# First q and k loads of a fused attention and FFN kernel: from cast loads on GpSimd to f32 loads on SyncE and ScalarE

## The chip, the cores and the metric

The kernel runs on one core of a Trainium2 chip. Its time is in microseconds (us) of the device. The times given are the median of several executions; the profile is of one further execution, whose own time stands beside its span.

## The reference

Windowed attention over 8 batches of 8 heads with 576 tokens of 64 elements, and a feed-forward network (FFN) with a squared ReLU on its output. Heads 0 to 3 look back over 32 tokens, heads 4 to 7 over every fourth token of the last 128.

```python
def _attn_ref(q, k, v):                    # q, k, v: (8, 8, 576, 64) float32
    scores = scale * np.matmul(q, k.transpose(0, 1, 3, 2))
    rel = pos[:, None] - pos[None, :]
    mask_plain = (rel >= 0) & (rel < 32)
    mask_dil = (rel >= 0) & (rel < 128) & (rel % 4 == 0)
    scores = np.where(masks[None], scores, -1000000000.0)   # plain: heads 0-3, dilated: 4-7
    attn = np.exp(scores - np.max(scores, axis=-1, keepdims=True))
    attn = attn / (np.sum(attn, axis=-1, keepdims=True) + 1e-09)
    return np.matmul(attn, v)

x = attn_out.transpose(0, 2, 1, 3).reshape(4608, 512)
h = np.maximum(x @ w_in, 0.0)              # w_in: (512, 2048)
out = h * h @ w_out                        # w_out: (2048, 512)
```

## The kernel before, in words

All matmuls are in bf16. The FFN works through 4608 tokens in eleven chunks, four of 256 tokens and then seven of 512. A chunk has "groups": `g1` multiplies x by pieces of w_in (line 673), takes the ReLU on ScalarE (L684) and the square on VectorE (L685); `g2` multiplies by w_out (L708), copies the sum out of PSUM (L714) and stores it (L647, SyncE). The attention of a batch is cut into small steps, by pair of heads `e` (0 to 3: two heads each, pairs 0 and 1 plain, 2 and 3 dilated), which stand between the FFN groups of the batch before.

The order of the work is written out by hand. The string `PROGRAM` (L21) holds codes, cut by `|`: the codes of the first stretch run before the first FFN group, those of stretch g + 1 after group g. Nothing else reorders instructions: each engine executes its own in the order in which they are issued here.

The codes that matter:

- `L0:q001` is `load_qk` of batch 0, part 0 (tokens 0 to 255), pairs 0 and 1: one load of q and one of k (L161). `L0:q023` is pairs 2 and 3, `q1..` part 1 (tokens 256 to 575), `L0:v..` are loads of v (L178 to L197), `i0` to `i3` the four pieces of w_in (L770), `o0` to `o3` of w_out (L775). All of these are on GpSimd's queue, which casts f32 to bf16 on the way.
- `T10` transposes q and k of pair 1, part 0, on TensorE into PSUM (L505); `T20q`, `T20k` one of them; `C10a` copies the result to SBUF, q's half on ScalarE (`a`) or VectorE (`v`) at L519 and k's on VectorE (L520), or both at once (L512).
- `B` puts the mask as a bias into PSUM (L535), `S` adds the scores (L554), `E` takes the exponential (L562, for part 1 with a mask on VectorE, L565), `P` multiplies by v (L592), `D` sums the rows (L608), `L` and `X` give the reciprocal on ScalarE (L615, L618), `M` writes the quotient to `xT`, the FFN's input (L625).
- `w9` and `W6` are idle matmuls (L475): so many products of a zeroed tile `idle` with itself into a spare PSUM tile, `w` with 512 columns, `W` with 256. `W5+11` puts them into the PSUM tile of S11 instead, ahead of the exponential that reads it.
- `h` casts v of the plain heads (part 0) from f32 into `vbd[0]` (L797). Those rows come by four plain f32 loads, two on SyncE and two on ScalarE (L739), into a tile that VectorE first writes one column of (L736), after the masks `mk` have landed (L723, ScalarE's first load).
- `u`, `m` build masks on ScalarE, `n` and `z` zero halves of `kbd` and `vbd`.
- Later codes such as `3o1` or `4k0` are steps of a batch: batch 3, the part-0 product with v (`o`) of pair 1; batch 4, k's copies (`k`) of pair 0, with `l` and `h` for one half each and `a` for ScalarE.

Four copies on ScalarE (L734) zero the unused halves of `vbd[0]`: two of 64x1152 and two of 64x128. `xx[0]` and `xx[1]` hold transposed q and k by batch; `xx[1]` is first written for batch 3. PSUM has four buffers of the pool `ps_f` ("pf"), two of `ps_a` ("pa"), one each of "po" and "pd". The FFN's first accumulators are taken from "pf" after S21, S31, S01 and S11.

The first FFN groups run in the order 0, 1 (w_in's first piece), 2, 3 (second piece), 16 (first piece, the second chunk), 4, 5 (third piece), 17 to 21, 6, 7 (fourth piece), and so on.

Of the kernel before, what the change touches and what calls it, by code (L numbers as in the profile page):

```python
# [12 lines left out]
RES = 4  # L13
# [5 lines left out]


PROGRAM = (  # L21
    "L0:q001 L0:q023 L0:q101 L0:q123 L0:v0d L0:i0 L0:v1dr L0:i1 L0:v1p L0:i2 L0:i3 L0:o0 L0:o1 L0:o2 L0:o3 "
    "L1:q00123 z y L1:v0dp L1:q10123 L1:v1dpr w9 T00 C00a T10 C10a B00 B10 W2 S00 E00 B20 W1 S10 E10 u B30 W3 "
    "T20q W6 T20k C20v T30 C30v h W3 S20 E20 W2 S30 E30 T01 C01v T11 C11a W4 P00 P10 D00 D10 L00 T21 C21v T31 "
    "C31v W6 X00 M00 P20 P30 D20 D30 L20 X20 M20 S21 S31 E21 E31 S01 S11 W5+11 E01 E11 | | P21 P31 D21 D31 L21 "
    "X21 M21 L31 X31 M31 | | P01 P11 D01 D11 L01 X01 M01 L11 X11 M11 | | | | | | | | | | | | | m n | | | | | "
    "L2:q00123 L2:q10123 | 1q1 1q3 | 1q2f 1k2f | 1k1a 1v3 | 1a2 | 1v2 1k0a 1q0v | 1o2 | 1a0 1a1 | 1k3 1o0 1o1f "
    "| 1a3 1Q0 | 1K0 1o3 | 1Q1 1K1 | 1Q2 | 1b0 | | 1Q3 1K2 L2:vwpdr L3:q00123 L3:q10123 | L2:x | | 2q0 | | 2k0 "
    "1V2 | 1b2 1p0 | 1b1 1V3 1K3 | | 1p2 1p1f | 2a0 1b3 | 2k1l 2o0 1p3f 2b0 2k1h | 2q1 2k2 L3:x | | 2q2 2p0 "
    "L3:vwpdr 2a1 | | | 2b1 | 2o1 2a2 2v2 2q3 | | 2p1f | 2k3 | 2b2 2o2 | 2v3 | 2a3 2p2f L4:q10123 | 2b3 2o3 | "  # L30
    "3k1 | 2p3 | 3q1v L4:q00123 | 3k0l | 3a1 | 3k0h | | 3o1 3k2l | 3q0 | 3k2h 3v2 | | | 3a0 | 3b1 3k3 | | | "
    "3p1 L4:x 3q2 L4:vwpdr | | 3b0 | 3a2 3q3 3o0 4k0 | | | 3o2 3b2 | | 3p0 3v3 | 4q1 3a3 | 3p2 4q2 4q0 | "
    "L5:q10123 3b3 | 3o3 | 4k1 | | L5:q00123 3p3 4k2 4k3 4a0 L5:vwpdr | | | 4b0 | | 4q3 | | 4o0 | | | 4a2 4v2 "
    "| 4b2 | 4a3 L5:x 4a1 | 4o2 | | | 4p2 L6:q00123 4v3 | | 4b1 | | 4p0 | | 4p1 | 5q0 5k0 | 4b3 | | | | 4o1 | "
    "| 5k2 L6:q10123 4o3 | 5q2 5k1 | | 4p3 | 5q1 |"
)


# [25 lines left out]
def kernel(  # L64
# [85 lines left out]
    def staged(b: int, nm: str):  # L150


        t = rb[STAGE[b]][nm]
        return t[:, :].rearrange("p (a h x) -> p a h x", h=H, a=2)
# [324 lines left out]
    def first_step(code: str):  # L479
# [54 lines left out]
            for x, (to, rhs) in enumerate(adds):  # L534
                nc.tensor.matmul(to, ident, rhs, start=(x == 0), stop=False, skip_group_check=True)  # L535
        elif what == "S":
            ps = ps_f.tile([P, 512], f32, name="pf") if part else first["S", e, part]
            if part == 0:
                pts[e] = p_pool.tile([P, NB * 96], bf16, name="pt")
            bl = blocks(0, e, part)  # L540
# [109 lines left out]
    def ffn_groups(tk0: int, nt: int):  # L650

        early = NT <= tk0 <= 2 * NT
        h2 = h2_pool.tile([P, NF, NT], bf16, name="h2T")
        per = NT // nt
        kts = (0, 2, 1, 3) if tk0 >= NT else (0, 1, 2, 3) if tk0 == 0 else (2, 3, 0, 1)
        cut = 3 if tk0 >= NT else 2
        cur, acc = {}, {}

        cuts = [(0, nt)] if tk0 // RING == (tk0 + nt - 1) // RING else [(0, -tk0 % RING), (-tk0 % RING, nt)]

        def mm1(u, ks):
            if u not in acc:
                acc[u] = ps_f.tile([P, NT], f32, name="pf")
            for x in range(per):
                f = per * u + x
                piece = max(y for y in range(len(w_in_sb)) if w_cuts[y] <= P * f)
                c0 = 512 * (f // 4) + f % 4 - w_cuts[piece]
                for kt in ks:  # L670
                    for y0, y1 in cuts:
                        t0 = (tk0 + y0) % RING
                        nc.tensor.matmul(  # L673
                            acc[u][:, nt * x + y0 : nt * x + y1],
                            w_in_sb[piece][:, kt, c0 : c0 + 509 : 4],
                            xT[:, kt, t0 : t0 + y1 - y0],
                            start=(kt == kts[0] and x == 0 and y0 == 0),
                            stop=(kt == kts[-1] and x == per - 1 and y1 == nt),
                            skip_group_check=True,
                        )  # L680
            if ks[-1] != kts[-1]:
                return
            hv = h2[:, per * u : per * u + per, 0:nt]
            nc.scalar.activation(hv, acc[u][:, :].rearrange("p (x n) -> p x n", x=per), ACT.Relu)  # L684
            nc.vector.tensor_tensor(out=hv, in0=hv, in1=hv, op=ALU.mult)  # L685

        def g1(i):
            if i < 2 and tk0 < NT:
                for u in range(2):
                    mm1(u, kts[2 * i : 2 * i + 2])  # L690
            elif i < 2 and early:
                for u in (2 * i, 2 * i + 1):
                    mm1(u, kts[:cut])
            elif i < 4 and early:
                for u in (2 * i - 4, 2 * i - 3):
                    mm1(u, kts[cut:])
            else:
                mm1(i, kts)

        def g2(m, part):  # L700
            last = tk0 + P * (m + 1) == NTOK
            if part == 0 or last and part == 2:
                cur[m] = ps_f.tile([P, DM], f32, name="pf")

            c0, c1 = (DM // 2 * (part // 2), DM // 2 * (part // 2 + 1)) if last else (0, DM)
            f0, f1 = (NF // 2 * (part % 2), NF // 2 * (part % 2 + 1)) if last else (4 * part, 4 * part + 4)
            for f in range(f0, f1):
                nc.tensor.matmul(  # L708
                    cur[m][:, c0:c1], h2[:, f, P * m : P * m + P], w_out_sb[:, f, c0:c1],
                    start=(f == 0), stop=(f == NF - 1),  # L710
                )
            if f1 == NF:
                osb = osb_pool.tile([P, DM], f32, name="osb")
                nc.scalar.copy(osb[:, c0:c1], cur[m][:, c0:c1])  # L714
                for x in (c0, DM // 2) if c1 - c0 == DM and tk0 == NTOK - NT else (c0,):
                    store(osb, tk0 + P * m, x, DM // 2 if x < min(c1, DM // 2) and tk0 == NTOK - NT else c1)

        return [lambda i=i: g1(i) for i in range(NF // per)] + [
            lambda m=m, part=part: g2(m, part) for m in range(nt // P) for part in range(4)
        ]  # L720

# [5 lines left out]
        nc.vector.memset(t[64:128, :, :, 0:64], 0.0)  # L727

    nc.vector.memset(idle[:, :], 0.0)
    for es, bs in ((slice(0, NE // 2), slice(0, NB)), (slice(NE // 2, NE), slice(8, NB))):  # L730
        for hl in range(2):
            to = vbd[0][64 * hl : 64 * hl + 64, es, bs, 64 - 64 * hl : 128 - 64 * hl]
            none = idle[64 * hl : 64 * hl + 64, 0:64].unsqueeze(1).unsqueeze(1).broadcast_to(list(to.shape))
            nc.scalar.copy(to, none)  # L734
    plain = osb_pool.tile([P, DM], f32, name="osb")[:, :].rearrange("p (e i d) -> p e i d", e=2, d=D)
    nc.vector.tensor_copy(plain[:, :, 0, 0:1], mk[:, 0:2].unsqueeze(2))  # L736
    for e, engine in enumerate((nc.sync, nc.scalar)):
# [47 lines left out]
    def run(code):  # L785
        if code == "y":
            for nm in "qk":
                nc.gpsimd.memset(staged(1, nm)[64:80, 0, :, :], 0.0)
                nc.gpsimd.memset(staged(2, nm)[64:80, 0, 0 : H // 2, :], 0.0)
        elif code == "z":  # L790
            nc.gpsimd.memset(vbd[1][0:64, :, :, 64:128], 0.0)
            nc.gpsimd.memset(vbd[1][64:128, :, :, 0:64], 0.0)
        elif code in "mu":
            masks(int(code == "u"))
        elif code == "h":
            for rows in sides:
                nc.vector.tensor_copy(vbd[0][rows, 0:2, 0:4, rows], plain[rows, :, :, :])  # L797
        elif code == "n":
            zero_halves(kbd)
            zero_halves(vbd[0][:, NE // 2 :, 0:8, :])  # L800
        elif code[0] in "wW":
            n, _, at = code[1:].partition("+")
            turn(int(n), 512 if code[0] == "w" else 256, [int(x) for x in at])
        elif code[0] in "TCBSEPDXM" or code[0] == "L" and code[2:3] != ":":
            first_step(code)
        elif code[0] != "L":
            step(int(code[0]), code[1:])
        else:
            b, what, part, which = int(code[1]), code[3], code[4:5], code[5:]
            if what == "q":  # L810
                load_qk(b, None if part == "w" else int(part), [int(e) for e in which])
            elif what == "x":
                cross_all(b)
            elif what == "v":
                load_v(b, [0, 1] if part == "w" else [int(part)], which)
            else:
                (load_w_in if what == "i" else load_w_out)(int(part))
# [67 lines left out]
```

## Time and profile before

| | |
|---|---|
| median of 7 runs | 310.26 us (309.8 to 312.5) |
| the profiled execution's own time | 311.11 us |
| its span | 309.3 us |
| TensorE matmuls busy | 300.5 us (97%), 2545 |
| TensorE weight loads busy | 188.0 us (61%) |
| VectorE busy | 195.4 us (63%) |
| ScalarE busy | 196.6 us (64%) |
| GpSimd busy | 94.0 us (30%) |
| DMA | 35.05 MB moved, mean 113 GB/s |
| chain that ended last | PE 85%, DMA 5%, GpSimd 2%, VectorE 2%, ScalarE 2% |

The busy times are unions over the span; engines work side by side, so they don't add up to it. PE is TensorE, PEld its weight loads, DVE VectorE, ACT ScalarE, POOL GpSimd, SP SyncE; a `q` behind an engine (ACTq, SPq) marks its queue issuing a load. A line of the timeline has the start and the length in us, engine, source line, operation and tiles, and in brackets how long the engine had stood idle before and what ended that. A line of the windows has the stretch, its length, the busy time of each engine with its instructions, the granted clock of TensorE, the mean share of the 16 DMA engines in use and the GB/s that they wrote. Loads with a cast write half of the bytes that they read.

### The profile page before, as it was taken

What the parts mean: (1) busy time and instruction counts of PE and PEld (TensorE: products, weight loads), DVE (VectorE), ACT (ScalarE), POOL (GpSimd) and SP (SyncE); (2) the same over time, 40 slices, a digit from 0 to 9 for tenths busy, and PEclk for the clock granted to TensorE, in tenths of its full rate; (3) what the DMA queues carried; (4) which work ended last, traced back from release to release, by engine and by line L of the source; (5) the groups of instructions that cost most, each with busy time, mean ns of one, the idle gap of its engine ahead of it and who ended that gap; (6) DMA issues with size and microseconds to landing.
All of it is one profiled execution on the core that took longest, in us unless ns stands there. A gap on an engine that the chain in (4) does not pass through costs nothing.

```text
span 309.3 us, 6792 instructions
## 1 busy us (share of the span) xinstructions
PE 300.5 (97%) x2545; PEld 188.0 (61%) x2577; DVE 195.4 (63%) x637; ACT 196.6 (64%) x421; POOL 94.0 (30%) x138
## 2 busy tenths in 40 slices
PE   7998999999999999999999999999999999999995
PEld 3788756868755555555599555555555555445544
DVE  1555566998988979975798469946995334104400
ACT  7587658859869765795388547854686456216611
POOL 8679785564236254601551051000000000000000
PEclk9999999999999999999999999999999999999999
DMA  7999999999999989999799985601200210121012
GB/s 108 197 169 212 204 134 183 175 128 224 154 110 202 159 130 187 152 137 173 104 127 135 154 125 87 107 11 59 68 3 0 70 69 0 32 72 34 2 53 83
DMA packets 80288, 35.05 MB, mean 113 GB/s; under 512 B 49920, under 2 KB 75648, under 8 KB 80256
## 3 DMA queue, kind: packets, MB, share of 16 engines
q0 software_dynamic: 46592, 18.23, 52.2%
q1 hardware_dynamic: 32976, 16.06, 28.4%
q8 instruction: 20, 0.33, 0.5%
q10 hardware_dynamic: 688, 0.33, 0.5%
q14 instruction: 12, 0.10, 0.1%
HBM read 36.90 MB, written 9.44 MB: 150 GB/s over the span
## 4 chain that ended last, share of the span: by engine, by line
PE 85%; DMA 5%; POOL 2%; DVE 2%; ACT 2%; issue 2%; ACTq 0%; POOLq 0%
PE pf L708 38%; PE pf L673 38%; DMA w_in<-in_moe_w_in_dram 5%; PE po L421 3%; PE pd L423 2%; PE pa L312 2%; PE pa L318 1%; PE pa L236 1%; POOL qb L161 1%; POOL kb L161 1%; DVE qT L256 1%; ACT rec L425 1%; ACT rec L426 1%; DVE kbd L260 1%; DVE xT L436 0%
## 5 line engine op out<-in xcount | busy, mean ns | idle before, releaser
L673 PE MATMUL pf<-xT,w_in 128*128 128x256 bf16 (+1 forms) x758 | 132.0, 325 | 1.4 <-DMA w_in<-in_moe_w_in_dram 0.9
L708 PE MATMUL pf<-w_out_sb,h2T 128*128 128x512 bf16 (+1 forms) x570 | 130.7, 373 | 1.2
L673 PEld LDWEIGHTS <-w_in 128*128 128x128 bf16 x768 | 82.3, 114 | 36.0 <-DMA w_in<-in_moe_w_in_dram 1.2
L684 ACT ACTIVATE h2T<-pf 128x512 bf16<-128x512 f32 x144 | 83.7, 597 | 25.3 <-PE pf L673 24.6
L708 PEld LDWEIGHTS <-h2T 128*128 128x128 bf16 x592 | 54.3, 98 | 53.5
L685 DVE TENSOR_TENSOR h2T<-h2T 128x512 bf16<-128x512 bf16 x144 | 58.0, 422 | 39.9 <-ACT h2T L684 38.7
L714 ACT COPY osb<-pf 128x512 f32<-128x512 f32 (+1 forms) x37 | 21.2, 572 | 43.7 <-PE pf L708 37.8
L436 DVE TENSOR_TENSOR xT<-po,rec 128x288 bf16<-128x288 f32 (+2 forms) x51 | 23.1, 454 | 32.0 <-ACT rec L426 31.5
L178 POOL DMA_DIRECT2D vbd<-in_v_dram x36 | 25.7, 733 | 41.3 <-PE pd L423 37.7
L425 ACT ACTIVATE rec<-pd 128x288 f32<-128x288 f32 (+2 forms) x51 | 21.0, 411 | 23.0 <-PE pd L423 23.0
L322 ACT ACTIVATE pt<-pa 128x352 bf16<-128x352 f32 (+6 forms) x56 | 27.6, 499 | 6.6 <-PE pa L312 3.7
L426 ACT ACTIVATE rec<-rec 128x288 f32<-128x288 f32 (+2 forms) x56 | 24.8, 444 | 1.8
L421 PEld LDWEIGHTS <-vbd 128*128 128x128 bf16 x286 | 17.1, 97 | 9.8 <-issue 0.7
L256 DVE COPY qT<-xx 64x288 bf16<-64x288 bf16 x84 | 21.0, 250 | 1.1
L191 POOL DMA_DIRECT2D vd<-in_v_dram x24 | 14.5, 617 | 16.9 <-DMA kb<-in_k_dram 9.6
L260 DVE COPY kbd<-xx 64x288 bf16<-64x288 bf16 x40 | 18.8, 471 | 0.6
L161 POOL DMA_DIRECT2D qb<-in_q_dram x18 | 12.9, 717 | 18.9 <-DMA xx<-qb 17.2
L421 PE MATMUL po<-pt,vbd 128*128 128x32 bf16 (+3 forms) x256 | 17.5, 198 | 0.4 <-DVE xT L436 0.4
L423 PE MATMUL pd<-pt,mk 128*128 128x32 bf16 (+6 forms) x150 | 15.9, 204 | 0.0
L197 POOL DMA_DIRECT2D vbd<-in_v_dram x16 | 9.7, 609 | 12.6 <-PE pd L423 5.1
L161 POOL DMA_DIRECT2D kb<-in_k_dram x18 | 12.7, 707 | 1.1 <-DMA kb<-in_k_dram 0.6
L312 PE MATMUL pa<-qT,kbd 128*128 128x96 bf16 (+2 forms) x146 | 12.2, 201 | 0.1
(95 smaller groups left out, 235.4 us busy)
## 6 DMA issues: line engine op xcount, KB each, us to landing
out_dram<-osb SPq DMA_DIRECT2D x18, 128.0 KB, 2.7
qb<-in_q_dram POOLq DMA_DIRECT2D x7, 320.0 KB, 7.2
kb<-in_k_dram POOLq DMA_DIRECT2D x7, 320.0 KB, 9.3
vd<-in_v_dram POOLq DMA_DIRECT2D x32, 64.0 KB, 7.1
w_in<-in_moe_w_in_dram POOLq DMA_DIRECT2D x4, 512.0 KB, 8.2
w_out_sb<-in_moe_w_out_dram POOLq DMA_DIRECT2D x4, 512.0 KB, 12.8
qb<-in_q_dram POOLq DMA_DIRECT2D x7, 256.0 KB, 7.4
kb<-in_k_dram POOLq DMA_DIRECT2D x7, 256.0 KB, 9.1
```

Of the source, the lines that this page charges most:

```text
L161: nc.gpsimd.dma_start(t[0:n, part, hs, :], src[b, hs, t0 : t0 + RES * n, :].rearrange("h (p r) d -> p h (r d)", r=RES))
L178: nc.gpsimd.dma_start(dst[rows, e, i0:i1, rows], v[b, 2 * e + hl, 64 * i0 : 64 * i1, :].rearrange("(i p) d -> p i d", p=64),)
L256: copy(qT[rows, e, :, m0 : m0 + n].rearrange("p (c j) m -> p j c m", j=2)[:, jj, :, :], src)
L322: nc.scalar.activation(pt[:, off : off + n], ps[:, 0:n], ACT.Exp, scale=SCALE)
L421: nc.tensor.matmul(oo, vb[:, e, i, :], rh, start=(x == 0), stop=(x == len(mms) - 1), skip_group_check=True)
L425: nc.scalar.activation(rec[:, 0:n], d[:, 0:n], ACT.Ln)
L426: nc.scalar.activation(rec[:, 0:n], rec[:, 0:n], ACT.Exp, scale=-1.0)
L436: nc.vector.tensor_tensor(out=tok, in0=o if o is o3 else o[:, 0:n], in1=rec if o is o3 else rec[:, 0:n], op=ALU.mult)
L673: nc.tensor.matmul(acc[u][:, nt * x + y0 : nt * x + y1], w_in_sb[piece][:, kt, c0 : c0 + 509 : 4], xT[:, kt, t0 : t0 + y1 - y0], start=(kt ...
L684: nc.scalar.activation(hv, acc[u][:, :].rearrange("p (x n) -> p x n", x=per), ACT.Relu)
L685: nc.vector.tensor_tensor(out=hv, in0=hv, in1=hv, op=ALU.mult)
L708: nc.tensor.matmul(cur[m][:, c0:c1], h2[:, f, P * m : P * m + P], w_out_sb[:, f, c0:c1], start=(f == 0), stop=(f == NF - 1),)
```

## The change

- The first loads of batch 0, `L0:q001` (q and k, pairs 0 and 1, part 0), are taken out of GpSimd's queue. In their place four plain f32 loads, of two heads each, go to the still unused `xx[1]`: q's two on SyncE, k's two on ScalarE. Casts (`c00`, `c10` on VectorE for q, `c01`, `c11` on ScalarE for k) bring them to where the cast loads wrote.
- One of four zero copies stays on ScalarE; three become memsets on VectorE (`g`, after `C10a`).
- Idle matmuls: `w9` becomes `w7`; `W4` and the second `W6` go; `W5+11` becomes `W2+31`.
- S01 and S11 run before X00 and take their PSUM from "pa"; E01 and E11 come before P20.
- In the middle, `3a1`, `3o1`, `3q2`, `3k3` and `4q1` stand up to nine groups elsewhere (stretches 67 to 91); `4k0` is cut in two halves, both on ScalarE, and stands later.
- The copy of the last row block out of PSUM is shared by ScalarE and VectorE; the stores of two more row blocks are cut in two halves of columns.

```diff
-    "L0:q001 L0:q023 L0:q101 L0:q123 L0:v0d L0:i0 L0:v1dr L0:i1 L0:v1p L0:i2 L0:i3 L0:o0 L0:o1 L0:o2 L0:o3 "
-    "L1:q00123 z y L1:v0dp L1:q10123 L1:v1dpr w9 T00 C00a T10 C10a B00 B10 W2 S00 E00 B20 W1 S10 E10 u B30 W3 "
-    "T20q W6 T20k C20v T30 C30v h W3 S20 E20 W2 S30 E30 T01 C01v T11 C11a W4 P00 P10 D00 D10 L00 T21 C21v T31 "
-    "C31v W6 X00 M00 P20 P30 D20 D30 L20 X20 M20 S21 S31 E21 E31 S01 S11 W5+11 E01 E11 | | P21 P31 D21 D31 L21 "
...
+    "L0:q023 L0:q101 L0:q123 L0:v0d L0:i0 L0:v1dr L0:i1 L0:v1p L0:i2 L0:i3 L0:o0 L0:o1 L0:o2 L0:o3 L1:q00123 z "
+    "y L1:v0dp L1:q10123 L1:v1dpr w7 c00 c01 T00 C00a c10 c11 T10 C10a g B00 B10 W2 S00 E00 B20 W1 S10 E10 u "
+    "B30 W3 T20q W6 T20k C20v T30 C30v h W3 S20 E20 W2 S30 E30 T01 C01v T11 C11a P00 P10 D00 D10 L00 T21 C21v "
+    "T31 C31v S01 S11 X00 M00 E01 E11 P20 P30 D20 D30 L20 X20 M20 S21 S31 W2+31 E21 E31 | | P21 P31 D21 D31 "
...
-            ps = ps_f.tile([P, 512], f32, name="pf") if part else first["S", e, part]
+            if part:
+                pool, nm = (ps_f, "pf") if dil else (ps_a, "pa")
+                first["S", e, part] = pool.tile([P, 512], f32, name=nm)
+            ps = first["S", e, part]
...
-                nc.scalar.copy(osb[:, c0:c1], cur[m][:, c0:c1])
-                for x in (c0, DM // 2) if c1 - c0 == DM and tk0 == NTOK - NT else (c0,):
-                    store(osb, tk0 + P * m, x, DM // 2 if x < min(c1, DM // 2) and tk0 == NTOK - NT else c1)
+                mid = (c0 + c1) // 2 if last else c1
+                nc.scalar.copy(osb[:, c0:mid], cur[m][:, c0:mid])
+                if last:
+                    nc.vector.tensor_copy(osb[:, mid:c1], cur[m][:, mid:c1])
+                for x in (c0, DM // 2) if c1 - c0 == DM and tk0 + P * m >= NTOK - NT - 256 else (c0,):
+                    store(osb, tk0 + P * m, x, DM // 2 if x < min(c1, DM // 2) and tk0 + P * m >= NTOK - NT - 256 else c1)
...
     nc.vector.memset(idle[:, :], 0.0)
-    for es, bs in ((slice(0, NE // 2), slice(0, NB)), (slice(NE // 2, NE), slice(8, NB))):
-        for hl in range(2):
-            to = vbd[0][64 * hl : 64 * hl + 64, es, bs, 64 - 64 * hl : 128 - 64 * hl]
+    raw = [
+        xx[1][0:64, x, 0 : 4 * RES * D * 2].bitcast(f32).rearrange("p (h d) -> p h d", h=4) for x in range(2)
+    ]
+    for e in range(2):
+        for x, (src, engine) in enumerate(((q, nc.sync), (k, nc.scalar))):
+            engine.dma_start(
+                raw[x][:, 2 * e : 2 * e + 2, :],
+                src[0, 2 * e : 2 * e + 2, 0:256, :].rearrange("h (p r) d -> p h (r d)", r=RES),
+            )
+
+    def zeros(hl, es, bs, act):
+        to = vbd[0][64 * hl : 64 * hl + 64, es, bs, 64 - 64 * hl : 128 - 64 * hl]
+        if act:
             none = idle[64 * hl : 64 * hl + 64, 0:64].unsqueeze(1).unsqueeze(1).broadcast_to(list(to.shape))
             nc.scalar.copy(to, none)
+        else:
+            nc.vector.memset(to, 0.0)
+
+    zeros(0, slice(0, NE // 2), slice(0, NB), True)
...
+        elif code == "g":
+            zeros(1, slice(0, NE // 2), slice(0, NB), False)
+            for hl in range(2):
+                zeros(hl, slice(NE // 2, NE), slice(8, NB), False)
+        elif code[0] == "c":
+            e, x = int(code[1]), int(code[2])
+            hs = slice(2 * e, 2 * e + 2)
+            (nc.scalar.copy if x else nc.vector.tensor_copy)(staged(0, "qk"[x])[0:64, 0, hs, :], raw[x][:, hs, :])
```

The new loads and the one zero copy stand ahead of the v loads of L739 on SyncE and ScalarE; the casts stand in the first stretch of `PROGRAM`, behind them.

## Prediction

> **What bounds the kernel now.** I read the page first, then the chain that ended last in order of time, then TensorE's waits and its timeline, then half-microsecond windows of the start.
>
> ```profile
> PE   7998999999999999999999999999999999999995
> DMA  7999999999999989999799985601200210121012
> ```
>
> TensorE is full from the third slice (about 23 us) to the last; only the start and the very end have room. The chain shows where the full part begins and what lets it begin:
>
> ```profile
> 5.74 0.63 POOL kb L161
> 6.37 1.19 POOL vd L184 x2
> 7.56 0.26 issue
> 7.82 8.74 DMA w_in<-in_moe_w_in_dram
> 16.57 0.28 issue
> 16.85 1.30 POOL vbd L178 x2
> 18.15 7.63 DMA w_in<-in_moe_w_in_dram
> 25.83 9.80 PE pf L673 x88
> ```
>
> Until 25.83 us the chain is GpSimd's queue of loads and their landing; the third piece of w_in (group 4 of the FFN needs it) lands at 25.78, and from there TensorE carries the chain. The feed-forward groups that need only pieces one and two are done before:
>
> ```profile
> 23.88 1.04 PE L673 MATMUL pf<-xT,w_in 128*128 128x256 bf16 x8
> 25.83 9.80 PE L673 MATMUL pf<-xT,w_in 128*128 128x256 bf16 x88 [0.91 <-DMA w_in<-in_moe_w_in_dram]
> ```
>
> So TensorE is ready at 24.92 and waits 0.91. The time is set by the later of two clocks: when w_in's third piece lands (25.78) and when TensorE has done all that comes before (24.92). Whatever the change does to the start counts only through that later one. After it, the windows of 10 us from 30 to 300 show TensorE busy 9.84 to 10.00, but for 9.56 in 110 to 120.
>
> **Queue of loads.** GpSimd starts at 1.25 with heads 0 to 3 of q and k and issues a load every 0.63; GpSimd waits before w_in's first piece for a q load ("0.26 <-DMA qb", landing 7.5), before the next for k and so on: the eighth load before must have landed. All but the first eight are paced by the DMA engines, not by GpSimd. What the engines moved at the start:
>
> ```profile
> 1.50:2.00 0.50, 0.50 (x3) 0.22 (x2) 0.00 (x0) 0.50 (x1) 0.50 (x2) 1.00 0.31 52
> 2.00:2.50 0.50, 0.50 (x3) 0.20 (x2) 0.00 (x0) 0.49 (x2) 0.50 (x1) 1.00 0.77 243
> 2.50:3.00 0.50, 0.50 (x3) 0.15 (x1) 0.00 (x0) 0.50 (x1) 0.50 (x2) 1.00 0.42 107
> 3.00:3.50 0.50, 0.50 (x2) 0.15 (x1) 0.17 (x1) 0.49 (x2) 0.50 (x2) 1.00 1.14 73
> 4.00:4.50 0.50, 0.50 (x3) 0.08 (x1) 0.00 (x0) 0.49 (x2) 0.50 (x2) 1.00 1.45 193
> 5.50:6.00 0.50, 0.50 (x25) 0.44 (x24) 0.00 (x0) 0.27 (x2) 0.50 (x2) 1.00 0.86 88
> 9.00:9.50 0.50, 0.50 (x25) 0.45 (x24) 0.11 (x1) 0.50 (x3) 0.34 (x1) 1.00 1.41 206
> ```
>
> The last column is GB/s written. Nothing moves before 1.5; mk is alone until 3.0; q and k reach full pace at 4.0 (193), fall to 88 in 5.5 to 6.0, and recover by 8.5.
>
> **The change, the loads.** Two of GpSimd's loads go (2 x 0.63 = 1.25 us of issue; all behind them can be issued 1.25 earlier). Four f32 loads of 128 KB come, two on SyncE and two on ScalarE. ScalarE's mk was issued at 0.78 and its bytes start in the window 1.5 to 2.0; the new ones should start as soon. By 4.5 us the old kernel had moved mk (0.20 MB) and 0.5 x (73 + 167 + 193) = 0.22 MB of bf16, which is 0.43 MB read as f32. The new one has the engines at work from 1.7 to 4.5, 2.8 us. At mk's 243 GB/s (a copy without cast, alone) that is 0.68 MB, less mk 0.48 of q and k: ahead by 0.05 MB, or 0.13 us at the later pace (195 GB/s written, 390 read). At 390 it is 1.09, less mk 0.89: ahead by 0.46 MB, 1.18 us. I take 0.9: with up to five loads in flight on three queues it is nearer to the loaded rows at 4.0 than to mk alone. Everything later in the queue is unchanged in bytes and order, so w_in's third piece lands 0.9 (0.13 to 1.18) sooner, at 24.9.
>
> Against this speaks the Trainium skill ("DMA: Bandwidth & Descriptors", section "Issuing engines are not separate DMA queues"): loads issued from several engines run on the same 16 DMA engines, and only issue time is saved. The rows agree from 3.5 on; before 1.5 they show the engines idle, which is where the 0.9 comes from. By the rule alone the gain would be next to nothing, and the time that of rival C.
>
> **The casts and TensorE's clock.** Two casts on VectorE (64x512 f32 to bf16; the row L797 has 0.42 each) and two on ScalarE (rows of 128x512: 0.58). In program order ScalarE's casts stand behind its two v loads (L739), which wait for VectorE's L736, which waits for mk. Before:
>
> ```profile
> 2.04 2.31 ACT L734 COPY vbd<-idle 64x1152 bf16<-64x1152 bf16 x2
> 3.46 1.40 ACTq L739 DMA_DIRECT2D osb<-in_v_dram  x2
> 4.36 0.60 ACT L734 COPY vbd<-idle 64x128 bf16<-64x128 bf16 x2
> 5.73 0.65 ACT L519 COPY xx<-pa 128x256 bf16<-128x256 bf16 x2 [0.76 <-PE pa L505]
> ```
>
> The issue of 1.40 ends at 4.86, 5.16 if mk lands 0.3 later beside the new loads. If it holds the cast back: cast to 5.5 or 5.8, k half of T00 (0.3) to 5.8 or 6.1, then C00a (0.38), the second cast (0.58), T10's k half (0.3): T10 ends at 7.1 to 7.4, against 5.95 now, 1.2 to 1.5 late. If it holds nothing, the cast starts when k has landed, about 3.7, and T10 ends some 0.6 sooner than now. Three groups of idle matmuls behind T10 go: W4, W6 and three of W5, 13 of 0.108 (W6: six in 0.83, one alone 0.28) = 1.4. Held back, TensorE is ready at 24.92 + 1.2 to 1.5 - 1.4 = 24.7 to 25.0; not held, at about 23. Both are near or before w_in's 24.9. I take held back: program order. Start of group 4 about 24.95, gain 0.9.
>
> w9 to w7 costs nothing in itself: TensorE waited for q at 4.65 anyhow. ScalarE loses three zero copies (1.15 + 2 x 0.30), VectorE gains memsets: the 64x1152 uint32 row has 1.02, half the size 0.51, two small at 0.17, 0.85 in all, while VectorE idles (its idle before L512 is 2.5); without that cover C20v, and with it S20, would be 0.85 late. S01 and S11 move to the other PSUM pool and ahead of X00: they free the FFN's first accumulators from waiting for E21 (17.00), which again helps only TensorE's clock.
>
> **Middle.** Groups 67 to 91 shift 3a1, 3o1, 3q2, 3k3, 4q1 by one to nine places, and give half-steps of 4k0 to ScalarE (4 x 0.48 = 1.9 us off VectorE). They lie between about 120 and 160, where TensorE is busy 39.72 of 40 us: nothing to win. The dearest wait of that kind is the 0.38 at 118.44 (po for VectorE's xT), ahead of the edited groups; I cost it at 0, with 0.4 lost or 0.2 won as ends.
>
> **End.** The last copy (128x256) takes 0.37, 128x512 takes 0.58; half of 256 by that slope is 0.27, VectorE's half beside it. 0.1 won (0 to 0.2). The stores of two earlier row blocks are split in two: SyncE issues one in 0.41 (median), its queue waits for ScalarE most of the time there, so 0 with the next copy's cover of 2.9 us.
>
> **Sum.** 0.9 + 0 + 0.1 = 1.0 us off the span of 309.3. The profiled execution took 311.11, 1.8 more than its span and 0.85 over the median; the shift is laid on the median: 310.26 - 1.0 = 309.2.
>
> **Rivals.** *A, the slow stretch goes too.* From 4.5 to 6.5 the engines write 119, 109, 88 and 119 GB/s, against 190 later, though GpSimd issues without waiting: 0.16 MB or 0.85 us lost, just when v's small rows come in on two queues beside q and k. With half of q and k already there, that may vanish. Then w_in lands at 24.0, and if ScalarE's issue doesn't hold the cast, so is TensorE: gain 1.85, 308.4. Against it: the v loads remain and q and k of heads 4 to 7 take the others' place. 0.36.
>
> *B, TensorE becomes late: slower.* Idle weight loads take 0.15 up to 3.61 and 0.10 at 3.98: TensorE runs at half speed for its first 2.9 us of idle matmuls (0.43 for 512 columns; later 0.108 for 256). w7 ends at 4.05, and with the casts held back only sixteen small transposes come in the next 2 us. If TensorE falls back to half speed until about 12, 17 idle matmuls cost 0.11 more each and the bias and score matmuls some 0.7: 2.5. Ready at 25.0 + 2.5 = 27.5, 1.7 after 25.83: 311.9. It decides from a ready time of 25.83, and shows as slower from 27.4. For it: the order of the casts; against: warm rows already at 3.98. 0.15.
>
> The skill ("TensorE: Matmul & The Clock Gate", "Part 1: The HAM clock gate") has full speed come after a busy window of about 3.4 us and go after an idle one; seven cold matmuls of 0.43 are 3.0, short of it, nine are 3.9. By that rule alone w7 would be risky; the row shows the step after 2.9.
>
> *C, the bytes are what counts.* Moved loads take the engines' time all the same (the lower end, 0.13): 310.1. 0.09.
>
> **How the numbers follow.** Forecast 0.40, of which 0.04 beyond 1.55 us (its upper ends). 0.5% is 1.55 us, about what a measurement of this kernel can tell from no change. Faster 0.36 + 0.04 = 0.40; same 0.36 + 0.09 = 0.45; slower 0.15. Range: down to A with the upper end of the loads (308.0), up to the half of B (311.0), leaving out about 2 in 10.
>
> **What would show it.** In the new profile: bytes of q and k from 1.7 on; L770's second pair issued near 17.2 instead of 18.15; the long L673 block starting at 24.9 to 25.0 instead of 25.83, and what ended the wait before it (DMA: loads; none: TensorE). ScalarE's casts at 4.9 or later if held back, at 3.7 if not. Weight loads of 0.10 or 0.15 between 4 and 9. TensorE busy as before from 120 to 160. I am wrong if the block starts after 25.8 or before 24.5, or if TensorE shows new waits after it.

## The result, and the profile after

The changed kernel takes 313.24 us (median of 12 runs, 312.7 to 317.59); the kernel before, on the same chips, 310.69 us (31 runs). The ratio is 1.0091, 95% interval 1.0068 to 1.0114: slower, where the prediction had 1.0 us gained and a range that ended at 311.0. The ratio, and with it the loss of 2.8 us, compares the means without the slowest run of the changed kernel (317.59), which fell in a slower state of the chip; the medians differ by 2.55. The profiled execution took 312.8 us with a span of 311.0 (before: 309.3). Three pieces make up the 1.7 between the two spans:

| piece | before | after | difference |
|---|---|---|---|
| start of the span to group 4's first matmul (the 41st with w_in) | 25.83 | 27.71 | +1.9 |
| from there to the end of TensorE's last matmul | 280.18 | 279.80 | -0.4 |
| from there to the end of the span | 3.29 | 3.51 | +0.2 |

Lines have moved by a few numbers: the FFN's L673 and L708 are L676 and L711, the copy L714 is L718 (with VectorE's part in L720), L739 (v loads) is L759, L770 (w_in) is L790. The new f32 loads are L741, the casts L822.

The rows of the page, 40 slices of 7.8 us:

```profile
PE   5899999999999999999999999999999999999995
DMA  8999999999899799995699975702200210121022
```

The first slice of TensorE went from 7 to 5; nothing else in the row changed. The chain that ended last, in order of time, in the first 30 us (start, duration, what):

```profile
1.17 5.51 DMA xx<-in_k_dram
...
6.70 0.63 ACT kb L822
...
7.37 0.44 PE pa L505 x8
...
7.83 0.38 ACT xx L519
...
8.24 0.42 DVE xx L520
8.66 0.34 DVE qb L822
...
9.04 0.63 PE pa L505 x12
9.68 0.70 PE pf L535 x4
...
27.00 3.06 PE pf L676 x28
```

Before, the chain ran through GpSimd's queue and w_in. Now it is the new k load: issued at 1.17, landed 5.51 us later, then its cast, the k half of T00 (7.37), the copy C00a on ScalarE and then VectorE, the second cast of q (c10) behind that copy in VectorE's queue, and T10, after which TensorE carries the chain. The timeline of the same stretch (start, duration, engine, line, operation, count, and what ended the idle time before):

```profile
1.17 1.44 ACTq L741 DMA_DIRECT2D xx<-in_k_dram  x2
...
3.84 0.42 DVE L822 CAST qb<-xx 64x512 bf16<-64x512 f32 x1
3.91 1.29 SPq L759 DMA_DIRECT2D osb<-in_v_dram  x2
3.91 1.54 ACTq L759 DMA_DIRECT2D osb<-in_v_dram  x2
...
6.70 0.62 ACT L822 CAST kb<-xx 64x512 bf16<-64x512 f32 x1 [2.90 <-DMA xx<-in_k_dram]
...
7.37 0.42 PE L505 MATMUL pa<-mk,kb 64*64 64x64 bf16 x8 [2.63 <-ACT kb L822]
...
9.61 0.77 PE L535 MATMUL pf<-mk 128*128 128x288 bf16 x4
```

ScalarE's cast waits 2.90 us for k and starts 1.25 us after the issue of the v loads has ended (3.91 + 1.54 = 5.45). B00 (L535) starts at 9.61, 3.74 later than before, and its four matmuls take 0.77 where they took 0.48. This is its line before:

```profile
5.87 0.48 PE L535 MATMUL pf<-mk 128*128 128x288 bf16 x4
```

TensorE is still at half speed there, and stays so until about 12.5. It had not come up before its wait for k either: the q half of T00, at 4.32, takes 0.42, where the one before, at 4.66, took 0.31. Later on TensorE waits no more for w_in:

```profile
24.18 1.91 PE L676 MATMUL pf<-xT,w_in 128*128 128x256 bf16 x16
...
26.83 10.65 PE L676 MATMUL pf<-xT,w_in 128*128 128x256 bf16 x96
```

The third piece was issued at 17.11 and landed at 24.44; group 4, at 27.71 inside the second line, is late because TensorE is. The account of TensorE's 2.8 us in the two profiles (ready at 27.71 against 24.92): B00 +3.7; from B00 to T20's q half 3.25 against 2.16, +1.1 (half speed); from there to the first FFN matmul (20.63 against 17.63) -1.8, most of it idle matmuls left out; from there to group 4 -0.2.

The windows of half a microsecond (the stretch and its length; busy PE, PEld, DVE, ACT, POOL; clock; DMA share; GB/s):

```profile
2.50:3.00 0.50, 0.50 (x3) 0.15 (x1) 0.00 (x0) 0.35 (x1) 0.50 (x2) 1.00 0.93 313
3.00:3.50 0.50, 0.50 (x2) 0.15 (x1) 0.03 (x1) 0.50 (x1) 0.50 (x2) 1.00 0.56 57
3.50:4.00 0.50, 0.50 (x2) 0.00 (x0) 0.50 (x2) 0.30 (x1) 0.50 (x2) 1.00 0.68 93
5.00:5.50 0.50, 0.00 (x0) 0.00 (x0) 0.00 (x0) 0.00 (x0) 0.50 (x2) 1.00 1.31 234
```

More is moved early (313 GB/s against 107 in the first of them), then there is a hole of 57 and 93 just when k is due. From 4.5 to 6.5 the engines move 177 to 288 GB/s, while TensorE waits for k and has nothing to do (0.00 from 5.0 to 5.5). The clock column says 1.00 all the time, though equal matmuls take nearly twice as long: the durations are the better witness here.

The end (timeline):

```profile
307.59 0.27 ACT L718 COPY osb<-pf 128x128 f32<-128x128 f32 x1 [1.48 <-PE pf L711]
307.89 0.29 DVE L720 COPY osb<-pf 128x128 f32<-128x128 f32 x1 [1.46 <-ACT osb L718]
```

The two halves go one after the other: 0.27 + 0.29 and a gap, 0.59 in all, where one copy took 0.37 before:

```profile
306.09 0.37 ACT L714 COPY osb<-pf 128x256 f32<-128x256 f32 x1 [1.38 <-PE pf L708]
```

### The profile page after: what moved, and what is told of

It reads as the page before. It is cut to its first block, busy times and chain, and to the rows that moved or that the text cites. A ratio compares the mean times of both kernels' runs of the same rounds, so it can differ in the third digit from the quotient of the medians.

```text
span 311.0 us, 6781 instructions
## 1 busy us (share of the span) xinstructions
PE 299.9 (96%) x2530; PEld 187.5 (60%) x2562; DVE 195.9 (63%) x640; ACT 197.8 (64%) x424; POOL 92.7 (30%) x136
## 4 chain that ended last, share of the span: by engine, by line
PE 89%; ACT 4%; DVE 2%; DMA 2%; issue 1%; ACTq 0%
PE pf L711 38%; PE pf L676 38%; PE po L421 3%; PE pd L423 2%; DMA xx<-in_k_dram 2%; PE pa L312 2%; PE pa L318 1%; PE pa L236 1%; ACT h2T L687 1%; PE pa L505 1%; PE po L475 1%; ACT pt L322 1%; ACT qT L256 1%; ACT rec L425 0%; PE pf L535 0%
## 5 line engine op out<-in xcount | busy, mean ns | idle before, releaser
L676 PE MATMUL pf<-xT,w_in 128*128 128x256 bf16 (+1 forms) x758 | 132.1, 325 | 0.7 <-DVE xT L628 0.2
L711 PE MATMUL pf<-w_out_sb,h2T 128*128 128x512 bf16 (+1 forms) x570 | 130.7, 373 | 1.2
L676 PEld LDWEIGHTS <-w_in 128*128 128x128 bf16 x768 | 82.4, 114 | 34.8 <-issue 0.3
L711 PEld LDWEIGHTS <-h2T 128*128 128x128 bf16 x592 | 54.3, 98 | 53.5
L718 ACT COPY osb<-pf 128x512 f32<-128x512 f32 (+1 forms) x37 | 21.0, 566 | 43.9 <-PE pf L711 35.9
L256 DVE COPY qT<-xx 64x288 bf16<-64x288 bf16 x84 | 20.4, 243 | 1.2
L260 DVE COPY kbd<-xx 64x288 bf16<-64x288 bf16 x36 | 16.9, 470 | 0.5
L312 PE MATMUL pa<-qT,kbd 128*128 128x96 bf16 (+2 forms) x146 | 12.2, 201 | 0.0
```

The costliest lines, as they stand in the source:

```text
L256: copy(qT[rows, e, :, m0 : m0 + n].rearrange("p (c j) m -> p j c m", j=2)[:, jj, :, :], src)
L676: nc.tensor.matmul(acc[u][:, nt * x + y0 : nt * x + y1], w_in_sb[piece][:, kt, c0 : c0 + 509 : 4], xT[:, kt, t0 : t0 + y1 - y0], start=(kt ...
L711: nc.tensor.matmul(cur[m][:, c0:c1], h2[:, f, P * m : P * m + P], w_out_sb[:, f, c0:c1], start=(f == 0), stop=(f == NF - 1),)
```

## The experiments

Theory at the start: k lands late and TensorE, idle meanwhile, stays at half speed; both make group 4 late. Rivals: it is the order on ScalarE (the cast behind the v loads' issue) alone; it is the shorter warm-up alone; it is GpSimd's loads beside the new ones. Ratios are against the kernel before on the same chip, with 95% intervals.

**1. The old loads of the first pairs again, all else as after.**

```diff
-    "L0:q023 L0:q101 ...
+    "L0:q001 L0:q023 L0:q101 ...
-    "... w7 c00 c01 T00 C00a c10 c11 T10 C10a g ...
+    "... w7 T00 C00a T10 C10a g ...
-    for e in range(2):
-        for x, (src, engine) in enumerate(((q, nc.sync), (k, nc.scalar))):
-            engine.dma_start(...)
```

> The changed kernel with its first q and k loads of pairs 0 and 1 back on GpSimd as cast loads; casts gone, all else as changed. Theory L (the k loads land late and TensorE stands still for them): T10 ends near 5.9 us instead of 9.7, the third piece of w_in lands near 25.8 again, the long feed-forward block starts within 0.2 us of that; with the middle's gain of about 0.5 and the end's loss of 0.2 some 310.4 us. Theory M (the rest of the edits costs it: fewer idle matmuls, memsets on VectorE, S01 and S11 earlier, the middle): it stays above 312.

309.79 us, 0.9984 [0.9971, 0.9998]. The loss is gone, so all of it comes by way of the loads and their casts. The timeline:

```profile
5.46 0.42 PE L505 MATMUL pa<-mk,kb 64*64 64x64 bf16 x8 [0.28 <-DMA kb<-in_k_dram]
...
6.24 0.77 PE L535 MATMUL pf<-mk 128*128 128x288 bf16 x4
...
23.82 8.36 PE L676 MATMUL pf<-xT,w_in 128*128 128x256 bf16 x75
```

B00 is back at 6.24, but at half speed (0.77). After seven idle matmuls TensorE had not come up to full speed: T00's q half at 4.76 takes 0.42 too, and half speed lasts until about 9.4. That costs at most 0.3 here: group 4 comes at 24.70, when TensorE gets to it, 0.29 behind w_in (24.41).

**2. TensorE kept busy while it waits, loads as after.** Two more idle matmuls ahead (w9), twenty between the halves of T00, ten before T10.

```diff
-    "... w7 c00 c01 T00 C00a c10 c11 T10 C10a g ...
+    "... w9 c00 c01 T00q W20 T00k C00a c10 c11 W10 T10 C10a g ...
```

> The changed kernel with w9 for w7, and 20 and 10 more idle matmuls of 256 columns where TensorE waits for k of pair 0 and for q of pair 1 (T00 cut into T00q, W20, T00k; W10 ahead of T10). Theory L alone: T10 still ends at 9.7 and the time stays at 313.2 (within 0.3). Theory H (the clock at half speed from 4.3 to 12.1 us is a part of the loss of its own): weight loads stay at 0.10 after 4.5, the stretch from T10's end to T20q shrinks from 3.2 to 2.1 us, and the time falls by about 1.1 us, to 312.1; what remains over the kernel before is the late load.

311.93 us, 1.0051 [1.0033, 1.0069]. Full speed from B00 on (2.04 us from B00 to T20's q half, against 3.25), and 0.40 of the 0.91% of loss back. In the profiled execution k landed later still:

```profile
7.94 0.62 ACT L822 CAST kb<-xx 64x512 bf16<-64x512 f32 x1 [4.14 <-DMA xx<-in_k_dram]
```

Group 4 came at 27.73 there, as late as in after, at full clock: that execution took 312.4, the longest of the four.

**3. GpSimd's loads 3.5 us later.** Its two zeroing memsets go ahead of them.

```diff
-    "L0:q023 L0:q101 ... L1:q00123 z "
+    "z L0:q023 L0:q101 ... L1:q00123 "
```

> The changed kernel with GpSimd's 4.1 us of memsets (z) ahead of its first load, so that its loads start after 5 us. Only the landings of the first loads are asked for. Theory G (k lands late because GpSimd's loads share the DMA engines from 3 us on): k of pair 0 lands near 3.7 instead of 6.7 and k of pair 1 near 4.4 instead of 7.9. Theory S (loads of ScalarE's queue, or a second load of any hardware queue, are slow by themselves): they land as late as before, above 6. The time itself gets worse either way, since w_in comes some 4 us later.

One run, 312.36 us (before: 310.37). The DMA view of the first 3 us (KB each, median us from issue to landing), first of after, then of this kernel:

```profile
xx<-in_k_dram ACTq DMA_DIRECT2D x2, 128.0 KB, 5.7
```

```profile
xx<-in_k_dram ACTq DMA_DIRECT2D x2, 128.0 KB, 4.2
```

Without GpSimd's loads beside them, k's first pair lands at 5.48 in place of 6.68, and the second at 6.13 in place of 7.92. So GpSimd's loads are part of the delay (1.2 to 1.8 us), not all of it: from 3.7, which was assumed, 1.8 remain. And now the other suspect comes into view (timeline):

```profile
4.87 1.54 ACTq L759 DMA_DIRECT2D osb<-in_v_dram  x2
...
6.44 0.62 ACT L822 CAST kb<-xx 64x512 bf16<-64x512 f32 x1 [2.64 <-DMA xx<-in_k_dram]
```

k is there at 5.48, but the cast starts at 6.44, just after the issue of the v loads ended (6.41). The profile names the DMA as releaser; by the times it was ScalarE's own queue.

**4. Only pair 0 as f32, k ahead of mk on ScalarE, both casts on VectorE, w9, the last copy undivided.**

```diff
-    "L0:q023 ... w7 c00 c01 T00 C00a c10 c11 T10 ...
+    "L0:q01 L0:q023 ... w9 c00 c01 T00 C00a T10 ...
+    for x, (src, engine) in enumerate(((q, nc.sync), (k, nc.scalar))):
+        engine.dma_start(raw[x][:, 0:2, :], ...)
     nc.scalar.dma_start(mk[:, :], mk_dram.ap())
```

> Only pair 0 comes as f32: its q on SyncE and its k on ScalarE ahead of mk, both cast by VectorE; pair 1 is the first cast load on GpSimd (64 KB each for q and k); w9 again; the last copy undivided; else as the changed kernel. Theories L and G: both f32 loads land before GpSimd's loads are under way, near 3.3, T00 ends near 5, T10 near 5.5; w_in's third piece lands about half as much sooner as in the changed kernel (25.1 to 25.3), TensorE is ready before it, and with the middle's 0.5 the time is 309.5, below the kernel before (310.7). Theory S: k of pair 0 lands above 5 and the time is above 311.

311.29 us, 1.0047 [1.0014, 1.0081]: a miss as a better version. It shows one thing: ahead of mk, k lands at 3.69, 2.9 us after its issue at 0.78, the time that the prediction had assumed. Its line in the DMA view:

```profile
xx<-in_k_dram ACTq DMA_DIRECT2D x1, 128.0 KB, 2.9
```

But mk then lands at 5.30 in place of 3.5, and the identity that every transpose needs comes with it; T00 starts at 6.03. B00 runs at full speed (0.48), and yet TensorE is at half speed from 8.3 to about 11.7.

**5. Experiment 1 with w9 in place of w7.**

```diff
-    "... w7 T00 C00a T10 ...
+    "... w9 T00 C00a T10 ...
```

> The loads-undone kernel (first loads as cast loads on GpSimd again) with w9 for w7. Theory H (seven idle matmuls leave the clock at half speed; nine bring it to full): weight loads of 0.10 from 4 us on, T10 ends near 5.9, from the first bias matmul to T20q 2.1 us instead of 3.3, and TensorE is ready for group 4 about 1.1 us sooner than with w7 (24.7), at 23.6; group 4 then starts when w_in's third piece lands (24.4 to 25.8). Time 309.2 to 309.8, no more than 0.4 below w7's 309.8 because the landing takes over. Theory N (w7 is enough, the clock fell for another reason): nothing changes in the first 10 us.

310.22 us, 0.9998 [0.9974, 1.0022]. The timeline:

```profile
5.78 0.48 PE L535 MATMUL pf<-mk 128*128 128x288 bf16 x4
...
25.46 6.74 PE L676 MATMUL pf<-xT,w_in 128*128 128x256 bf16 x60 [0.45 <-DMA w_in<-in_moe_w_in_dram]
```

With these loads, B00 has full speed behind nine idle matmuls (0.48) and half speed behind seven (0.77 in experiment 1). The time is the same, since w_in's landing takes over, and TensorE waits 0.45 for it. The clock costs only where TensorE is the later of the two. The number of idle matmuls doesn't fix the moment, though: experiment 8, with the same start as the kernel before and nine of them, has T00's q half at 0.42 still (5.02) and full speed only from about 5.5.

**6. The same with the last copy undivided.**

```diff
-                mid = (c0 + c1) // 2 if last else c1
-                nc.scalar.copy(osb[:, c0:mid], cur[m][:, c0:mid])
-                if last:
-                    nc.vector.tensor_copy(osb[:, mid:c1], cur[m][:, mid:c1])
+                nc.scalar.copy(osb[:, c0:c1], cur[m][:, c0:c1])
```

> The same with the last copy out of PSUM undivided on ScalarE, as in the kernel before. The two halves of the changed kernel ran one after the other (0.27, then 0.29 on VectorE): from TensorE's last matmul to the end of the span 3.5 instead of 3.3 us. Expected: 3.3 again, 0.2 less of the time than the run beside it, which the interval can't tell but the profile can; the best of the kernels so far, 309.0 to 309.6.

309.8 us, 0.9975 [0.9950, 1.0000]; from the last matmul to the end 3.57, with the divided copy (experiment 5) 3.79. The division costs 0.2: the last store lands 2.40 after the last matmul, with the divided copy 2.63. The kernel before has 3.29 in all; the other 0.28 lies behind that landing (2.36 there): 0.93 from the landing to the end before, 1.17 here. SyncE's closing waits end one by one in that stretch, some 0.06 us each, one of them before and in after, five here and in experiment 5. Why more are left wasn't tried.

**7. The halves of the last copy into two SBUF tiles, with two stores, to see what puts them in order** (loads and warm-up as in experiment 5).

```diff
+                    osb2 = osb_pool.tile([P, DM], f32, name="osb")
                     nc.scalar.copy(osb[:, c0:mid], cur[m][:, c0:mid])
-                    nc.vector.tensor_copy(osb[:, mid:c1], cur[m][:, mid:c1])
+                    nc.vector.tensor_copy(osb2[:, mid:c1], cur[m][:, mid:c1])
+                    store(osb, tk0 + P * m, c0, mid)
+                    store(osb2, tk0 + P * m, mid, c1)
```

> The same with the last copy in halves on ScalarE and VectorE into two tiles with a store each. If the shared tile makes VectorE wait for ScalarE, the halves now run side by side and TensorE's last matmul to the end takes 3.2 us (0.1 under the undivided copy); if PSUM's side does, VectorE still starts 0.3 after ScalarE and it takes 3.5.

311.1 us, 1.0011 [0.9979, 1.0043]. The timeline of its end has two such pairs:

```profile
305.46 0.27 ACT L720 COPY osb<-pf 128x128 f32<-128x128 f32 x1 [1.16 <-PE pf L711]
305.76 0.29 DVE L721 COPY osb<-pf 128x128 f32<-128x128 f32 x1 [11.39 <-ACT osb L720]
...
307.65 0.27 ACT L720 COPY osb<-pf 128x128 f32<-128x128 f32 x1 [1.92 <-DMA out_dram<-osb]
308.15 0.29 DVE L721 COPY osb<-pf 128x128 f32<-128x128 f32 x1 [2.10 <-ACT osb L720]
```

In the first pair VectorE, idle for 11.39 us, starts 0.03 after ScalarE's end, released by ScalarE's copy, though the two write different SBUF tiles; in the second both also waited for a buffer that a store was still reading. What is left that they share is the PSUM tile that both read.

**8. The kernel before, with only the middle of the order changed.**

```diff
-    "... 3k0l | 3a1 | 3k0h | | 3o1 3k2l | 3q0 | ...
+    "... 3k0l | | 3a1 3k0h | | 3k2l | 3o1 3q0 | ...
```

> The kernel before with the changed kernel's order of steps after the first group, nothing else. In the profiles group 4's first matmul to TensorE's last takes 280.2 us before and 279.3 to 279.8 in the changed kernel and its variants. Theory R (the new order of 3a1, 3o1, 3q2, 3k3, 4q1 and 4k0 brings that): 279.4 here too, time 0.3 to 0.8 below the kernel before. Theory T (it comes from where the start leaves the loads and VectorE against TensorE, not from the order): 280.2, time within 0.3.

309.9 us, 0.9967 [0.9938, 0.9997]. From group 4 to the last matmul 279.69 (before 280.18), and the wait of 0.4 us at 118 for VectorE's xT is not there. Its line before:

```profile
118.44 0.33 PE L421 MATMUL po<-pt,vbd 128*128 128x96 bf16 x5 [0.38 <-DVE xT L436]
```

The trace points at 4q1. Before, its four copies (L256) held VectorE from 116.25 for 1.37, and the xT that TensorE waited for came behind them, at 117.94. Here they come at 113.51, and that xT at 117.49. No run moved this step alone. The middle brings 0.5 us in the profiles, and 0.3% (1.0 us) in the times, with an interval that nearly reaches 1.

**9. As after, without the f32 loads: the casts read a zeroed tile** (parts 0 of pairs 0 and 1 of q and k are left out).

```diff
-            engine.dma_start(raw[x][:, 2 * e : 2 * e + 2, :], ...)
+    nc.vector.memset(raw[0][:, 0:2, :], 0.0)
```

> The changed kernel without its four f32 loads: the casts read one zeroed tile instead (q and k of pairs 0 and 1, part 0, are zero), so that nothing of them has to land. Theory L (the late landing is what costs it): TensorE's wait for the casts falls to what is left of the order. If ScalarE's two v loads hold its cast back, that cast starts where their issue ends (near 4.9 us), T00's k half at 5.5 and T10 ends near 7.3 to 7.6; if not, it starts before 4 and T10 ends near 5.5. Group 4 starts near 25.3 or 24.5; time 309.5 to 310.5, about 3 below the changed kernel. Theory O (the casts and their order alone cost it, landing or not): T10 ends after 9, time above 312.5.

312.34 us (310.93 to 315.74, four runs), 1.0105 [1.0042, 1.0169]. The profiled execution is the shortest, 310.93. Its timeline:

```profile
3.27 1.40 ACTq L754 DMA_DIRECT2D osb<-in_v_dram  x2
...
4.72 0.62 ACT L817 CAST kb<-xx 64x512 bf16<-64x512 f32 x1 [1.53 <-issue]
...
7.33 0.48 PE L535 MATMUL pf<-mk 128*128 128x288 bf16 x4
...
8.08 0.50 PE L557 MATMUL pf<-xx 64*64 64x96 bf16 x8
```

The cast has nothing to wait for, and still starts only when the v loads' issue ends (3.27 + 1.40 = 4.67): program order on ScalarE holds it back. T10 ends at 7.4, the end of the prediction's 7.1 to 7.4, but by another path: TensorE waits 1.25 for VectorE's second cast of q (c10, behind the copy L520), and not for ScalarE's second cast of k. Seven idle matmuls bring full speed here (0.31 for T00's k half at 5.39, 0.48 for B00), and TensorE loses it only after its waits of 0.85 and 1.25: the scores (L557) take 0.50, and half speed lasts from 7.7 to about 11.2. The time came out no better without the landing. The profile shows only how the shortest run went, with group 4 at 25.70, no later than before; where the longer runs lose their time was not profiled, and the interval of four runs is wide.

**10. After with w9, and k ahead of mk on ScalarE's queue.**

```diff
-    "... w7 c00 c01 T00 ...
+    "... w9 c00 c01 T00 ...
+            engine.dma_start(raw[x][:, 2 * e : 2 * e + 2, :], ...)
     nc.scalar.dma_start(mk[:, :], mk_dram.ap())
...
-            engine.dma_start(raw[x][:, 2 * e : 2 * e + 2, :], ...)
```

> The changed kernel with w9 and with the f32 loads ahead of mk on ScalarE's queue (k of pair 0, k of pair 1, then mk). Theory Q (place in the queue decides the landing): k of pair 0 lands near 3.7 and k of pair 1 near 4.5, against 6.7 and 7.9; mk lands late instead, near 5.5, and with it VectorE's L756, q's casts and the v loads; ScalarE's cast of k starts only after the issue of those v loads, near 7.4 although k landed at 3.7, so that T00's k half is no earlier than in the changed kernel (7.4 to 8.1). Theory G (GpSimd's loads decide): k of pair 0 lands above 5 all the same.

One run, 320.82 us (before: 309.81). The timeline:

```profile
7.69 0.17 DVE L756 CAST osb<-mk 128x2 f32<-128x2 bf16 x1 [6.68 <-DMA mk<-mask_patterns]
...
7.89 1.54 ACTq L759 DMA_DIRECT2D osb<-in_v_dram  x2
...
9.48 0.62 ACT L822 CAST kb<-xx 64x512 bf16<-64x512 f32 x1 [5.48 <-issue]
...
28.05 3.10 PE L676 MATMUL pf<-xT,w_in 128*128 128x256 bf16 x16
```

k lands at 3.71, and now mk, behind both k loads, lands at 7.67; the v loads wait for mk, and the cast of k for the v loads' issue: 9.48. Place in the queue decides, and moving the delay from k to mk is worse. TensorE is at half speed until about 31: sixteen FFN matmuls take 3.10, where after has 1.91. Why it stays down that long is open.

**11 and 12. Experiment 9 with TensorE kept busy (w9, three idle matmuls between the halves of T00, twelve before T10), and experiment 2 again, on one chip.**

```diff
-    "... w7 c00 c01 T00 C00a c10 c11 T10 C10a g ...
+    "... w9 c00 c01 T00q W3 T00k C00a c10 c11 W12 T10 C10a g ...
```

> The changed kernel without its four f32 loads (casts of a zeroed tile, q and k of pairs 0 and 1, part 0, are zero), with w9 and with TensorE kept busy while it waits for the casts (W3 ahead of T00's k half, W12 ahead of T10). Nothing lands late and the clock stays up; what is left of the change is the order of its casts. Theory H (with nothing late to land it was the half-speed clock that kept the kernel without the loads at 310.9 to 312.5): T10 ends at 7.4 as there, matmuls are at full speed from 5 us on, group 4 starts between 24.4 and 25.0, time 309.4 to 310.2, level with the kernel before. Theory O (order of the casts by itself): 311 or more.

> The filled kernel (f32 loads, w9, W20 and W10) once more, on the same chip as the kernel without the loads at full clock, since it had four runs. The difference between the two is the late landing of the f32 loads alone: T10's end at 9.7 to 10.5 against 7.4. Theory L: 1.5 to 2.2 us of time between them, this one at 311.5 to 312.2. If the landing counts for nothing: no difference.

Without the landing, and with TensorE kept busy: 310.19 us, 0.9986 [0.9967, 1.0004], level with the kernel before. With the landing, and kept busy: 311.76 us, 1.0039 [1.0021, 1.0057]. The two differ by 1.6 us, give or take 0.8, and the two kernels differ by 15 idle matmuls too. In the profiles TensorE is ready for group 4 at 25.27 and 26.35, both times behind w_in (23.55, 23.57); in experiment 11 half speed lasted to some 7 us even so. Keeping TensorE busy, with the landing, is the step from 1.0091 to 1.0039 or 1.0051 (experiments 12 and 2): 0.40 to 0.52%, which is 1.2 to 1.6 us; the account of the profile had 1.1 for half speed.

The two shares depend on the order in which they are taken away. With TensorE left idle, taking away the landing brought nothing that could be measured (experiment 9, 1.0105); with the landing gone, keeping TensorE busy is worth about 1.2% (1.0105 to 0.9986). What the runs show is that the loss is gone when both go (experiment 11), or when the loads are undone (experiment 1), and that either one alone leaves some 0.4% or more (experiments 2 and 12, and 9).

No version is clearly beyond the kernel before: the best two, experiments 6 and 8, have 0.9975 and 0.9967, with intervals that end at 1.0000 and 0.9997.

## Why the prediction was wrong

**The two clocks** were the right frame: the start of group 4 is the later of w_in's landing and of TensorE being ready. In experiment 5 the landing is the later one, in after TensorE is.

**"About 3.7" for k is the step that failed.** The prediction counted bytes for all loads together, and set k's landing by the engines being free from 1.7 on. It did not ask in which order they come. On ScalarE's queue k stands behind mk (192 KB): it was issued at 1.17, but in after its first packets move at 3.23, once mk's last are through (2.64), while q's on SyncE move from 2.48. Then it shares the engines with q and GpSimd's loads, and lands at 6.68. Experiments 4 and 10 have 3.69 and 3.71 with k ahead of mk, experiment 3 has 5.48 without GpSimd's loads. From there the sum was lost: T10 at 9.7 in place of 7.1 to 7.4. The bytes failed too: by 4.5 us some 0.37 MB of q and k had been read, less than the 0.43 before, where the forecast had 0.48 to 0.89.

**"I take held back"** was right as a mechanism (experiments 3, 9 and 10), and in after it didn't decide: the v loads held ScalarE only from 3.91 to 5.45, and k landed at 6.68.

**"w9 to w7 costs nothing in itself"** put the clock at nothing, and that failed too. The row read for it (weight loads of 0.15 until 3.61, 0.10 at 3.98) showed the step 2.9 us after the start of nine idle matmuls in one execution; it did not show that seven, with a wait behind them, would do. In after and in experiment 1 they don't: 0.77 for B00, where nine with the same loads as in experiment 1 have 0.48. Nor is the count a rule: seven sufficed in experiment 9, where the clock fell behind the waits, and nine did not in experiment 10. The rule of the Trainium skill ("TensorE: Matmul & The Clock Gate", "Part 1: The HAM clock gate") that was set against the row, a busy window of about 3.4 us before full speed and a fall after an idle one, agrees with these runs only in part: after and experiment 1 are as it says, but before came up after 2.9 us, and experiment 9 with seven. It was reason enough not to put w7 at nothing.

**Rival B was the true case**, with 0.15. Its ready time of 27.5 came near the 27.71 by luck, through two errors that nearly cancel: 2.5 us of half clock was too much (1.1 in the profile, 1.2 to 1.6 by the times), and the lateness taken for the casts too small (1.2 to 1.5, where B00 is 3.7 late). Its time, 311.9, is 1.3 short of the 313.24. By its own point of decision it came out: ready over 27.4, and slower. The 1.4 us for idle matmuls left out was about right (-1.8 for the whole stretch they stood in).

**The loads' 0.9.** w_in's third piece landed 1.34 sooner in after, and its second pair was issued at 17.11, near the 17.2 that was forecast. But it scatters by more than that: the six profiled kernels with the old cast loads have 24.35 to 27.22 (mean 25.5), the five with all f32 loads 23.38 to 25.30 (mean 24.3; in one of them GpSimd's loads start 3.5 us later). The term is neither shown nor refuted; it was not what set the time. This is why rivals A and C can't be judged by the time: both speak of a landing that TensorE no longer waits for. A's slow stretch did go (234 GB/s at 5.0 to 5.5, against 109), but a new hole came at 3.0 to 4.0 (57 and 93).

**Middle and end.** "Nothing to win" in the middle was some 0.5 us too low. The prediction put stretches 67 to 91 at 120 to 160 us; counted by the FFN's groups in the trace they run at about 93 to 118 (4k0's copies, for one, stand at 110.51 before). The wait at 118, costed at 0 as lying ahead of the edited groups, lies at their end, and it went (experiment 8). "VectorE's half beside it" was wrong: the halves queue, and the division costs 0.2 in place of the 0.1 won. The Trainium skill ("PSUM — Partial Sum Buffer", "PSUM bank collisions raise a hardware error") says that the compiler's scheduler adds a dependency between two instructions of different engines that touch the same bank and 32-partition quadrant, reads too; experiment 7 agrees, with VectorE's half released by ScalarE's, 0.30 us after its start, though nothing but the PSUM tile is shared.

## What to carry to other kernels

For a load that starts the whole machine, ask which bytes stand ahead of it on its queue and what stands ahead of its cast on the engine that issues it, not only whether the engines have room: the same 128 KB landed at 3.7 us as the first on its queue, and at 5.5 to 7.9 behind a load of 192 KB. Idle matmuls that look superfluous may be what brings TensorE to full speed or keeps it there: count a wait and the half-speed stretch behind it as one cost, don't take the moment of the step from one profile, and check whether TensorE is the later party at the next meeting point, because only then is it paid. Dividing a copy among two engines gains nothing while both read one PSUM tile.

## What was not expected of the hardware

- Half speed at the start lasted to 9.4 us (experiment 1), 12.5 (after) and, in experiment 10, 31, although the windows there show TensorE busy 15.81 of the 16 us from 12 to 28. In others it came after full speed: 7.7 to 11.2 (experiment 9), 8.3 to 11.7 (experiment 4), 12.2 to 22.5 (experiment 7). What sets the moments is open. The clock column of the windows read 1.00 at half speed.
- VectorE slows beside GpSimd's memsets: in experiment 3 the cast of q took 1.24 us and the one of mk's two columns 1.50, against 0.42 and 0.41 in after; both ended only after the last memset had (4.81).
- The landing of a load scatters by 1 to 3 us: experiments 2 and 12 are one and the same program, and its first load of k landed at 7.92 in one profile and at 6.09 in the other; w_in's third piece landed between 24.35 and 27.22 in six kernels with the same loads ahead of it.
